# Batch 3's scaled memory sums transposed by the DMA crossbar from ScalarE's queue

## The chip, the cores and the metric

The kernel runs on one core of a Trainium2 chip. The core has four compute engines that matter here: TensorE (matmuls, with weight loads beside them), VectorE, ScalarE and GpSimd. Each works through its own queue of instructions in order. DMA transfers are issued by instructions too, from the queues of SyncE (SP), GpSimd and ScalarE. TensorE writes to PSUM, eight banks of it; VectorE and ScalarE read results from there.

The metric is the device time of one execution in microseconds, the median over several runs.

## The reference

Attention with learned memory slots, followed by a gated feed-forward block. Per batch (8) and head (8), with 576 positions, head size 64 and 32 memory slots:

```python
a = softmax(phi)                                  # over the 32 slots
k_m = np.einsum('bhsm,bhsd->bhmd', a, k)          # sums over the positions
v_m = np.einsum('bhsm,bhsd->bhmd', a, v)
attn = softmax(q @ k_m.T / sqrt(64))              # over the 32 slots
x = (attn @ v_m), heads side by side              # 4608 tokens x 512
out = (silu(x @ w_gate) * (x @ w_val)) @ w_out    # 512 -> 1536 -> 512
```

## The kernel before

The order of all instructions is written out by hand: an engine executes what the program emits for it, in the order of emission. Work goes batch by batch. The memory sums of batch b+1 are computed in the middle of the feed-forward work of batch b.

For one batch of the later six:

- **Sums and scaling.** `kv_sum` (L230) makes the sums k_m and v_m of all heads in two PSUM banks; `kv_norm` scales them on VectorE with the reciprocals of the softmax denominators (L266) into `t_bkv`, three blocks of 128x128 in bf16.
- **Transposition.** `kv_T` (L279 on) makes `t_kT`, the three blocks transposed. For batches 2 and 3 TensorE transposes them through the bank `p_T` (L288) and VectorE copies the bank out (L289). For batches 4 to 7 a DMA transposes them, issued from SP (L284).
- **The u round.** `u_round` (L472) multiplies v_m, from `t_kT`, with columns of the two weights w_gate and w_val. ScalarE (L492) and VectorE (L496) convert the result into `t_U`. The first u round of batch b+1 that reads the new `t_kT`, `u_three(b + 1)`, is emitted late in the stretch of batch b.
- **Scores.** `scores` (L396) multiplies k_m, also from `t_kT`, with q transposed (`t_qT`), at the start of the stretch of batch b+1. `t_qT` of batch 3 and later comes from another transposing DMA on SP (`load_qT`, L117).
- **Slots.** A stretch has 24 slots, one for each of 12 blocks of 128 hidden columns and each half of the positions. In slot s, `gv_gate` multiplies the gate (two matmuls, `p_g`, L515) and ScalarE applies silu (L532, `t_sg`), which frees the gate's bank. Then follow the two matmuls of the value of slot s-1 (`p_v`, L515) and its product with the silu on VectorE (L538, `t_h`), which frees the value's bank.
- **Banks.** `bank` takes the PSUM bank at the front of a list and `done` puts it at the end, both at the time of emission. What TensorE waits for, when it writes to a bank, is thus fixed by the order in the program.
- **Output products.** `products` (L723) multiply `t_h` and sums of it with w_out.

`spread` orders a stretch. Each stream of items gets a first and a last key, its items are put evenly between them, and all are emitted in the order of the keys. The 24 slots have the keys 0.5, 1.5, and so on. The two items of `kv_items(b + 1)`, the sums and then `kv_T`, run from `KV` = 6 to 10, so they have the keys 7 and 9; `u_three(b + 1)` has 19.5:

```python
            streams += [
                (kv_items(b + 1, lambda: (u_item(b, 2, "aava")(), run(take(2)))), KV, KV + 4),
                ([lambda: (u_three(b + 1), run(take(2)))], 19, 20),
            ]
        spread(*streams)
```

So `kv_T(3)` is emitted in the stretch of batch 2, after slot 8 and before slot 9. The sums' item ends with a u round of batch 2 (`u_item(b, 2, "aava")`: four banks, three converted on ScalarE and one on VectorE) ahead of slot 7.

Of the kernel before, what the change touches and what calls it, by code (L numbers as in the profile page):

```python
# [14 lines left out]
def kernel(  # L15
# [19 lines left out]
    nc = tc.nc  # L35
# [39 lines left out]
    def bank(shape, dtype, name):  # L75
        tag = free.pop(0)
        t = ps.tile(shape, dtype, tag=tag, name=name)
        held[id(t)] = tag, t
        return t

    def done(*tiles):

        for t in tiles:
            free.append(held.pop(id(t))[0])
# [83 lines left out]
    ephis, rSs, bkvs, kTs, es, atts = {}, {}, {}, {}, {}, {}  # L168
# [109 lines left out]
    def kv_T(b):  # L278


        kTs[b] = att.tile([128, 3, 128], BF16, tag="kT", name="t_kT")
        t = bkvs.pop(b)
        if b > 3:
            nc.sync.dma_start_transpose(out=kTs[b], in_=t.rearrange("p n x -> p (n x)"))  # L284
            return
        p = bank([128, 3, 128], BF16, "p_T")
        for n in (2, 0, 1):
            nc.tensor.transpose(p[:, n], t[:, n], ident)  # L288
        nc.vector.tensor_copy(out=kTs[b], in_=p)  # L289
        done(p)  # L290

    def kv_items(b, beside=None):


        def run_sums():
            o = 2 * D
            behind = b in esums and b != 3
            own = beside and not behind
            if own:
                d = bank([128, NG], FP32, "p_S")  # L300
                kv_denominators(b, d)
                kv_reciprocal(b, d)
                done(d)
            p = [bank([128, CH], FP32, f"p_kv{g}") for g in range(NG)]
            if not (own or behind):
                kv_denominators(b, p[0][:, o:o + NG])
            kv_sum(b, p, (0, 1))
            if behind:
                beside()
                kv_denominators(b, p[0][:, o:o + NG])  # L310
            if not own:
                kv_reciprocal(b, p[0][:, o:o + NG])
            kv_norm(b, p)
            if beside and not behind:
                beside()

        return [run_sums, lambda: kv_T(b)]
# [795 lines left out]
```

## Time and profile before

| | us |
|---|---|
| median of 3 runs (lowest, highest) | 232.76 (232.63, 233.4) |
| the profiled execution | 232.59 |
| its span, first to last instruction | 230.8 |
| TensorE busy | 222.3 (96%) |
| VectorE busy | 184.8 (80%) |
| ScalarE busy | 171.6 (74%) |
| GpSimd busy | 145.1 (63%) |

The granted TensorE clock is full in all forty slices of the page. The costliest groups are those of the slots: the matmuls of the gates and of the values (L515), 77.0 and 76.9 us, the products on VectorE (L538), 81.7 us in 192 instructions, and the silus on ScalarE (L532), 73.2 us in 192.

In the profile PE is TensorE's matmul row, PEld its weight loads, DVE is VectorE, ACT ScalarE, POOL GpSimd and SP SyncE; a `q` behind an engine (SPq, ACTq) marks what its queue issues, such as a DMA. Instructions in a row of the same kind are merged where they are shown in order of time, so a merged line's duration runs from the first start to the last end. Matmuls are pipelined: one that is listed with 0.29 us can be followed by the next after 0.12. What counts is the distance between starts.

### The profile page before, as it was taken

The page shows a single profiled execution, that of the slowest core. Times are in us where ns is not written, and L with a number is a line of the kernel's source. Part 1 is how long each engine was busy: PE and PEld are TensorE (multiplying, and loading weights), DVE is VectorE, ACT ScalarE, POOL GpSimd, SP SyncE. Part 2 cuts the span into 40 slices and gives each one's busy share as a digit, 9 for nine tenths or more (in the row PEclk, how much of TensorE's full clock was granted, in tenths as well). Part 3 has the DMA queues.
Part 4 walks back from the last instruction along what each step waited for, and adds up shares of the span by engine and source line. Part 5 has one row for each costly group of instructions (what it writes and reads, how often), then busy time and mean ns, then how long its engine had stood idle before and what let it go on. Part 6 is the DMA issues. An engine that isn't in the chain of part 4 may idle for free.

```text
span 230.8 us, 7191 instructions
## 1 busy us (share of the span) xinstructions
PE 222.3 (96%) x2818; PEld 169.7 (74%) x2818; DVE 184.8 (80%) x423; ACT 171.6 (74%) x365; POOL 145.1 (63%) x197
## 2 busy tenths in 40 slices
PE   6997799999999999999999999999999999999993
PEld 2554476778887777878788787887788778878882
DVE  4056789999976799989997668998999899977832
ACT  2858898988547989968896658978898789677310
POOL 8422427998099759765977689464845394029291
PEclk9999999999999999999999999999999999999999
DMA  6999999999996993999299964996022602202024
GB/s 213 209 211 206 199 207 207 216 250 266 207 210 176 258 257 69 224 204 177 78 214 195 230 137 110 253 231 101 18 76 102 116 0 95 87 7 91 23 93 162
DMA packets 36546, 36.84 MB, mean 160 GB/s; under 512 B 14496, under 2 KB 30880, under 8 KB 36512
## 3 DMA queue, kind: packets, MB, share of 16 engines
q0 software_dynamic: 16272, 22.42, 52.7%
q1 hardware_dynamic: 19712, 13.37, 22.8%
q10 hardware_dynamic: 528, 0.59, 0.8%
q8 instruction: 22, 0.36, 0.6%
q14 instruction: 12, 0.10, 0.1%
HBM read 42.47 MB, written 9.44 MB: 225 GB/s over the span
## 4 chain that ended last, share of the span: by engine, by line
PE 87%; DMA 9%; POOL 2%; issue 0%; DVE 0%; POOLq 0%
PE p_os L723 21%; PE p_g L515 21%; PE p_v L515 20%; PE p_oc L723 10%; DMA W<-in_moe_w_val_dram 9%; PE p_oa L723 5%; PE p_u L472 5%; PE p_kv L230 2%; PE p_g L396 1%; POOL t_kv L99 1%; POOL t_kv L103 1%; PE p_q L383 1%; POOL t_q L108 0%; POOL W L138 0%; DVE t_q L339 0%
## 5 line engine op out<-in xcount | busy, mean ns | idle before, releaser
L538 DVE TENSOR_TENSOR t_h<-t_sg,p_v 128x288 bf16<-128x288 bf16 x192 | 81.7, 451 | 14.3 <-PE p_v L515 7.3
L515 PEld LDWEIGHTS <-t_U 128*128 128x128 bf16 x768 | 73.9, 98 | 21.2 <-issue 3.5
L532 ACT ACTIVATE t_sg<-p_g 128x288 bf16<-128x288 f32 x192 | 73.2, 424 | 17.2 <-PE p_g L515 11.4
L515 PE MATMUL p_g<-t_A,t_U 128*128 128x288 bf16 x384 | 77.0, 286 | 0.0
L515 PE MATMUL p_v<-t_A,t_U 128*128 128x288 bf16 x384 | 76.9, 286 | 0.0
L723 PEld LDWEIGHTS <-t_S 128*128 128x128 bf16 x384 | 37.3, 98 | 4.5 <-issue 0.2
L603 POOL TENSOR_TENSOR t_S<-t_h 128x512 bf16<-128x512 bf16 x17 | 19.6, 1154 | 27.7 <-DVE t_h L538 26.4
L723 PEld LDWEIGHTS <-t_h 128*128 128x128 bf16 x288 | 27.1, 98 | 8.6 <-issue 5.0
L492 ACT CAST t_U<-p_u 128x512 bf16<-128x512 f32 x51 | 27.0, 606 | 6.4 <-PE p_u L472 6.4
L723 PE MATMUL p_os<-t_T,t_S 128*128 128x256 bf16 x192 | 23.7, 273 | 0.0
L560 POOL TENSOR_TENSOR t_S<-t_S,t_h 128x512 bf16<-128x512 bf16 x17 | 19.6, 1155 | 1.3
L560 POOL TENSOR_TENSOR t_S<-t_h 128x512 bf16<-128x512 bf16 x16 | 18.4, 1152 | 0.0
L560 POOL TENSOR_TENSOR t_S<-t_h,t_S 128x512 bf16<-128x512 bf16 x16 | 18.4, 1151 | 0.0
L472 PE MATMUL p_u<-W,t_kT 64*32 64x512 bf16 (+1 forms) x416 | 15.3, 363 | 1.2 <-DMA W<-in_moe_w_val_dram 0.6
L870 PE MATMUL p_warm<-bones 128*128 128x512 bf16 x44 | 13.6, 450 | 1.7 <-DVE bones L892 1.7
L496 DVE CAST t_U<-p_u 128x512 bf16<-128x512 f32 x21 | 13.6, 683 | 1.9 <-PE p_u L472 1.9
L723 PE MATMUL p_os<-t_T,t_h 128*128 128x256 bf16 x96 | 14.8, 273 | 0.0
L452 DVE TENSOR_TENSOR t_A<-t_E,t_lz 128x576 bf16<-128x576 bf16 x16 | 11.4, 739 | 0.7 <-ACT t_lz L428 0.7
L723 PE MATMUL p_oc<-t_T,t_S 128*128 128x256 bf16 x96 | 11.9, 273 | 0.0
L723 PE MATMUL p_oa<-WO,t_h 128*128 128x256 bf16 x96 | 11.8, 273 | 0.0
L723 PE MATMUL p_oc<-WO,t_S 128*128 128x256 bf16 x96 | 11.8, 273 | 0.0
L723 PE MATMUL p_os<-WO,t_h 128*128 128x256 bf16 x96 | 11.8, 273 | 0.0
(108 smaller groups left out, 312.5 us busy)
## 6 DMA issues: line engine op xcount, KB each, us to landing
out_dram<-t_o SPq DMA_DIRECT2D x11, 512.0 KB, 3.3
t_kv<-in_k_dram POOLq DMA_DIRECT2D x8, 576.0 KB, 10.7
t_q<-in_q_dram POOLq DMA_DIRECT2D x8, 576.0 KB, 8.7
t_kv<-in_v_dram POOLq DMA_DIRECT2D x8, 576.0 KB, 15.1
t_phi<-in_phi_dram POOLq DMA_DIRECT2D x6, 576.0 KB, 8.5
out_dram<-t_o SPq DMA_DIRECT2D x10, 256.0 KB, 3.8
WO<-in_moe_w_out_dram POOLq DMA_DIRECT2D x3, 512.0 KB, 19.4
W<-in_moe_w_gate_dram POOLq DMA_DIRECT2D x2, 512.0 KB, 16.5
```

Of the source, the lines that this page charges most:

```text
L230: nc.tensor.matmul(p[g][32 * i:32 * i + 32, 0:n], lhsT=phi_of(b, g, j, i), rhs=kvs[b][64 * g:64 * g + 64, w0:w1, i, j * D:(j + 1) * D], st ...
L452: nc.vector.tensor_tensor(out=a, in0=es.pop((b, g)), in1=lzs.pop((b, g)), op=ALU.mult)
L472: nc.tensor.matmul(p[g][32 * i:32 * i + 32, o:o + n], lhsT=kTs[b][64 * g:64 * g + 64, 2, 32 * i:32 * i + 32], rhs=w_part(w, c, i, g, halve ...
L492: nc.scalar.copy(out=t, in_=p)
L496: nc.vector.tensor_copy(out=t, in_=p)
L515: nc.tensor.matmul(p[:, 0:HALF], lhsT=Us[b, c, g][:, o // 2, which, 128 * (o % 2):128 * (o % 2 + 1)], rhs=atts[b, g][:, r], start=(g == 0) ...
L532: nc.scalar.activation(out=sg, in_=gate[:, 0:HALF], func=AF.Silu)
L538: nc.vector.tensor_tensor(out=dst, in0=sg, in1=val[:, 0:HALF], op=ALU.mult)
L560: eng.tensor_tensor(out=out, in0=x, in1=y, op=ALU.subtract)
L603: eng.tensor_tensor(out=t[:, 0], in0=A21, in1=A22, op=ALU.add)
L723: nc.tensor.matmul(mine[home][:, u], lhsT=lhs(c, m, u), rhs=rhs(c, m), start=fresh and u == 0, stop=(k == 5), skip_group_check=u == 1 or n ...
L870: nc.tensor.matmul(p[:, 0:128 * a], lhsT=bones, rhs=x.to_broadcast([128, a, 128]) if a > 1 else bones, start=True, stop=True,)
```

## The change

One condition and one choice of queue in `kv_T`:

```diff
         kTs[b] = att.tile([128, 3, 128], BF16, tag="kT", name="t_kT")
         t = bkvs.pop(b)
-        if b > 3:
-            nc.sync.dma_start_transpose(out=kTs[b], in_=t.rearrange("p n x -> p (n x)"))
+        if b > 2:
+            (nc.sync if b > 3 else nc.scalar).dma_start_transpose(out=kTs[b], in_=t.rearrange("p n x -> p (n x)"))
             return
         p = bank([128, 3, 128], BF16, "p_T")
```

For batch 3 the three TensorE transpositions, the bank `p_T` and VectorE's copy go away, and one transposing DMA of the whole `t_bkv` into `t_kT` is issued from ScalarE's queue, at the same place in the order of emission. Batches 2 and 4 to 7 stay as they are.

## The prediction

> **What bounds the kernel now.** I read first the page's strip of busy tenths and its chain of waits, then the view of one tile for the tiles of the edit, then the instructions in order of time from 79 to 91 us, where the step of batch 3 runs, and last SP's own instructions in order of time. The strip and the chain:
>
> ```profile
> PE   6997799999999999999999999999999999999993
> PE 87%; DMA 9%; POOL 2%; issue 0%; DVE 0%; POOLq 0%
> ```
>
> TensorE is full from the sixth slice on, and the list of waits on TensorE between 31 us and the end is empty. So TensorE has no slack that could swallow a delay: a microsecond in which it waits comes out at the end in full, and so does one that it saves. ScalarE (74%) and VectorE (80%) follow it and matter only where they hold a PSUM bank that TensorE wants.
>
> The tiles of the edit (least, median and greatest duration in ns, then first and last start in us):
>
> ```profile
> L288 PE MATMUL p_T<-ident,t_bkv x6: 219/219/219, 61.9 to 82.2; 128*128 128x128 bf16 x6
> L284 SPq DMA_TRANSPOSE t_kT<-t_bkv x4: 1179/1690/2255, 107.0 to 182.1; - x4
> L289 DVE COPY t_kT<-p_T x2: 350/354/357, 62.3 to 83.4; 128x384 bf16<-128x384 bf16 x2
> DMA to landing us min/median/max: 2.6/3.6/4.5
> ```
>
> Half of L288 and of L289 belong to batch 2 and stay. The four DMA rows are batches 4 to 7 on SP's queue: the same instruction that batch 3 now gets on ScalarE's.
>
> The place, in order of time (start, duration, engine and line; several instructions in a row are merged):
>
> ```profile
> 81.08 1.56 ACT L492 CAST t_U<-p_u 128x512 bf16<-128x512 f32 x3 [0.78 <-PE p_u L472]
> ...
> 81.64 0.41 PE L515 MATMUL p_g<-t_A,t_U 128*128 128x288 bf16 x2
> ...
> 82.13 0.33 PE L288 MATMUL p_T<-ident,t_bkv 128*128 128x128 bf16 x3
> ...
> 82.30 0.41 PE L515 MATMUL p_g<-t_A,t_U 128*128 128x288 bf16 x2
> ...
> 82.51 5.54 ACT L532 ACTIVATE t_sg<-p_g 128x288 bf16<-128x288 f32 x13
> ...
> 84.26 0.41 PE L515 MATMUL p_g<-t_A,t_U 128*128 128x288 bf16 x2
> ...
> 87.78 0.84 PE L472 MATMUL p_u<-W,t_kT 64*32 64x512 bf16 x24
> ...
> 89.69 1.35 ACT L532 ACTIVATE t_sg<-p_g 128x288 bf16<-128x288 f32 x4
> ```
>
> The gate at 81.64 is that of slot 8, the one at 82.30 of slot 9, and from there a slot takes 0.49 us, so that 84.26 is slot 13. ScalarE runs late here: its three casts end at 82.64, and the silu of slot 7, whose gate TensorE began at 81.14, starts at 82.51. Four silus back to back take 1.35 us and one takes 0.45, so their pitch is (1.35 - 0.45) / 3 = 0.30: slot 7 at 82.51, slot 8 at 82.81, slot 9 at 83.10 (narrower windows of the same view show these starts singly). The line at 87.78 is the first reader of the new t_kT.
>
> **What is removed.** TensorE: the three transpositions take the time from 82.13 to 82.30, so 0.17 us, on the path. VectorE: the copy, 0.35 us; VectorE isn't what TensorE waits for here, so I cost it at nothing. Its cover is TensorE's own pace; without it the copy would be worth up to 0.35. The PSUM bank p_T drops out of the rotation, which only moves who inherits which bank; that is followed below.
>
> **What is added, and where.** The items of one stretch are sorted by keys; the transposition has key 9, between slot 8 (8.5) and slot 9 (9.5). On ScalarE's queue it stands after the silu of slot 8 and ahead of the silu of slot 9. Its input t_bkv is complete at 81.80 (four scalings from 80.81 in 0.99 us on VectorE), so it finds its data ready and starts when ScalarE's queue reaches it: no sooner than about 82.85, just after the silu of slot 8 starts, and no later than about 83.3, when that one has ended. I take 83.1, where the next silu stood. That an issue holds what is behind it on ScalarE is seen at the start of the trace:
>
> ```profile
> 0.73 0.49 ACTq L94 DMA_DIRECT2D t_phi<-in_phi_dram  x1
> 1.26 1.28 ACT L857 ACT_TABLE_LOAD   x1 [1.26 <-PEq L1097]
> ```
>
> How long the issue takes on ScalarE (call it D) no row shows; the plain load there took 0.49 us against 0.45 on SP, so the engines are close to alike. From below D is 0.49, by that load. From above I use SP's four rows:
>
> ```profile
> 61.62 5.99 SPq L117 DMA_TRANSPOSE t_qT<-t_q  x1
> ...
> 106.98 2.25 SPq L284 DMA_TRANSPOSE t_kT<-t_bkv  x1
> ...
> 132.90 1.91 SPq L284 DMA_TRANSPOSE t_kT<-t_bkv  x1
> ...
> 158.28 1.47 SPq L284 DMA_TRANSPOSE t_kT<-t_bkv  x1
> ...
> 182.12 1.18 SPq L284 DMA_TRANSPOSE t_kT<-t_bkv  x1
> ```
>
> 1.18 belongs to a nearly idle DMA (share 0.11), 2.25 to one full of transfers. At 83 us the DMA share is above 1.1, loads and stores together. The eighteen-block transposition at 61.62, also beside loads, took 5.99 us against 4.03 in the idle DMA at 176.39, 1.49 times as much; 1.18 x 1.49 = 1.76. I take the median, 1.69, nearest to that, and keep 1.18 and 2.25 as ends.
>
> **What is queued behind it and who waits.** Behind the issue stand the silus of slots 9, 10 and on. Each frees a gate's bank for TensorE and feeds a product on VectorE. No output matmul (L723) runs from 76.2 to 90.7 us, so all eight banks rotate, and a slot takes two (gate, and the value of the slot before): a gate gets the bank of the gate four slots earlier. Without p_T, the eight banks from gate 9 to value 11 come from the four of the u round (last cast 82.64), gates 7 and 8 (silus ahead of the DMA) and values 6 and 7 (multiplied by 83.44). None of these is held up. Gate 13 is the first that needs a silu behind the DMA, that of slot 9.
> - Silu 9 starts at 83.1 + D + 0.04 (SP's next instruction starts 0.04 to 0.1 after such an issue) and lasts 0.45. A follower starts 0.04 after its end (the product of slot 7 at 82.99, its silu's end 82.95). Gate 13 can start at 83.63 + D.
> - Before it started at 84.26; without the transpositions TensorE is there at 84.09.
> - Net: D - 0.63, or -0.17 where D is under 0.46. With D = 1.69: **+1.06 us**. With 1.18: +0.55; with 2.25: +1.62. The start of the issue moves each by -0.25 to +0.2.
>
> After gate 13 nothing stops TensorE again: ScalarE catches up with 0.30 per silu against 0.49 per slot, and VectorE's products at 0.37 back to back (three from 79.42 in 1.18 us) too. The removed 0.17 is in this sum, since TensorE reaches the wait sooner and waits longer.
>
> **The landing.** t_kT must be there for the u round at 87.78, then at 88.84. From 83.1 with 2.6 to 4.5 us it lands at 85.7 to 87.6. Beside loads the large transpositions landed after 9.5 to 11.0 us and late in the kernel, without them, after 6.2: at most 1.77 times. On the 2.6 and 3.5 us of the late small ones (mean 3.05) that makes 5.4, and 88.5. Cost nothing; the cover is 0.3 to 3 us, and is gone only if the transfer takes over 5.7. The extra 0.1 MB delays loads that end near 88.3 and are first used by the sums at 102.67: nothing.
>
> **Rules.** The page "DMA: Bandwidth & Descriptors" of the Trainium skill, under "Issuing engines are not separate DMA queues", says that issuing from several engines saves only the sequencer's time, usually small beside the DMA. The rows differ: 1.69 of 3.6 us is 47%. Were the issue small, the sum would be -0.17; by the rows it is +1.06. The same page, under "Silent corruption: two transposing streams in flight at once", speaks against this change: transposes from ScalarE and from SP must wait for each other's completion. In this trace both such waits would be over before they begin (the last rival but one has the times), and the sum by the rule is the same +1.06.
>
> **The rivals.**
> - *Not slower: the issue is short and the banks hide it.* Where D is below 1.33, the four slots of bank lead eat the stop and the sum is under +0.7. At D = 0.49 it is -0.14, so 232.6; at 1.18 with an early start +0.3, 233.1. For it: the load issued in 0.49, the idle row, and ScalarE's ring being empty, where SP's had the long t_qT just ahead in all four rows. Against: the full DMA, and 5.99 against 4.03 on an SP that had issued nothing since 0.74.
> - *The landing decides.* If three queues share the engines (loads, stores until about 85, the transposition) and it takes over 5.7 us, the u round waits. At 6.5 us it lands at 89.6, 0.8 after the need: 1.06 + 0.8, so 234.6. Decides from 88.84. Against: the longest of its kind was 4.5.
> - *The issue waits for something in flight on SP's queue* (stores until about 85): ScalarE stands from 83.1 to 85.1, and the sum is +3.1, so 235.8. Nothing in the trace of before asks for such a wait: SP's last transposition ahead of it, issued at 61.62, landed 9.5 us later, at 71.1, and the next is issued at 100.22.
> - *The change moves nothing*, the issue overlapping silus: -0.17, 232.6.
>
> **The numbers.** The profiled execution took 232.59 us with a span of 230.8, near the median 232.76 of the runs; the sum puts the span at 231.9 and the median at 232.76 + 1.06 = 233.8. Chances: forecast 0.66 (its own range +0.3 to +1.8, of which 0.08 falls within 0.3%), short issue 0.18 (0.15 within, 0.03 at the edge of faster), late landing 0.10, wait on SP's transfers 0.04, nothing 0.02. What a measurement of this kernel tells from no change is about 0.3%, 0.7 us. So slower 0.58 + 0.10 + 0.04 = 0.72, same 0.08 + 0.15 + 0.02 = 0.25, faster 0.03: no part of the edit has 0.7 us to give on TensorE. The range runs from 232.8, inside the short issue, to 235.0, inside the late landing.
>
> **What would show it.** A ScalarE issue near 83 us of 1.2 to 2.3 us; the silu of slot 9 near 84.8; a TensorE wait for a silu of about one microsecond at the gate of slot 13, near 84.1; no wait at the u round; everything later shifted by the same amount to the end. I am wrong if ScalarE's silus run on through the issue, if the stop sits at the u round, or if the shift is given back later.

## The result and the profile after

The changed kernel takes 236.29 us (median of 6 runs, 235.73 to 237.45) against 232.79 us before: 3.5 us slower. The ratio of the runs is 1.0165, with a 95% interval of 1.0148 to 1.0182. The forecast was 233.8, the range ended at 235.0. The sign was right, but not for the reason given: the stop that was forecast did not come. The loss is over three times the size that was worked out, and it lies in other places.

The profiled execution took 236.49 us with a span of 234.7. Its strip and chain:

```profile
PE   7967899999999995999999999999999999999992
PE 83%; DMA 12%; POOL 2%; issue 0%; DVE 0%; POOLq 0%
```

TensorE has a hole in the slice at 88 to 94 us, and DMA's share of the chain grew from 9% to 12%. From 31 us on the list of TensorE's waits, which was empty before, has one line (total, times, longest), and the chain that ended last has a new piece in the same place (start, duration):

```profile
PE p_u L472 <- DMA t_kT<-t_bkv: 2.4, 1, 2.4
```

```profile
82.85 7.87 DMA t_kT<-t_bkv
```

The tile of the edit (least, median, greatest duration in ns, then starts; the landing is that of this one DMA):

```profile
L284 ACTq DMA_TRANSPOSE t_kT<-t_bkv x1: 1281/1281/1281, 82.9 to 82.9; - x1
...
DMA to landing us min/median/max: 7.9/7.9/7.9
```

The same stretch in order of time:

```profile
81.78 1.56 ACT L492 CAST t_U<-p_u 128x512 bf16<-128x512 f32 x3 [0.78 <-PE p_u L472]
...
82.84 0.41 PE L515 MATMUL p_g<-t_A,t_U 128*128 128x288 bf16 x2
82.85 1.28 ACTq L284 DMA_TRANSPOSE t_kT<-t_bkv  x1
...
83.22 0.74 ACT L532 ACTIVATE t_sg<-p_g 128x288 bf16<-128x288 f32 x2
...
84.24 4.36 ACT L532 ACTIVATE t_sg<-p_g 128x288 bf16<-128x288 f32 x11 [0.27 <-PE p_g L515]
...
84.80 0.41 PE L515 MATMUL p_g<-t_A,t_U 128*128 128x288 bf16 x2
...
87.98 0.41 PE L515 MATMUL p_v<-t_A,t_U 128*128 128x288 bf16 x2
...
90.77 0.84 PE L472 MATMUL p_u<-W,t_kT 64*32 64x512 bf16 x24 [2.37 <-DMA t_kT<-t_bkv]
```

Two things are to be seen. The issue (L284) begins at 82.85, while ScalarE's last cast still runs (to 83.34) and two silus ahead of it in the queue have not begun; they execute at 83.22 to 83.96, during the issue. And gates 9 to 13 go on in steps of 0.49 us (82.84 to 84.80): no stop at slot 13. The stop is at the u round, which waits from 88.40 to 90.77.

Matching TensorE's instructions of the two traces one by one gives the account of the profiled execution:

| stretch | later than before by, us | added there |
|---|---|---|
| start, up to 27 us (landings of the first loads) | 0.68 | 0.68 |
| from there to slot 8 | 0.71 | 0.03 |
| after the place of the three transpositions | 0.54 | -0.17 |
| after the u round's wait | 2.98 | 2.44 |
| last matmul | 2.99 | 0.01 |
| end of the span | 3.9 | 0.9 |

The 0.7 us at the start differ from run to run: in the profiles of the first three experiments below TensorE is 0.02, 0.23 and 0.05 us later at that point. The step of 2.44 and the 0.9 at the end are new with the change. The 0.9 us at the end shows in SP's waits, as a longer wait for the landing of the last store. Before:

```profile
SPq L1108 <- DMA out_dram<-t_q: 0.5, 1, 0.5
```

After:

```profile
SPq L1108 <- DMA out_dram<-t_q: 1.4, 1, 1.4
```

The store itself lands 2.1 us after its issue in both. What differs is its turn. In these traces the DMAs of SP and ScalarE use eight semaphores in rotation (a semaphore counts the landings), and at the end SP goes through all of them in a fixed order. Before, the last store had the last one, so the others were checked while it was under way. One DMA more puts it on the first, and the other checks and the close follow only after it: SP stands there until 232.87, and the span ends at 234.7, 1.8 us later, against 0.9 us from the landing (229.9) to the end before.

### The profile page after: what moved, and what is told of

Read it like the earlier page. It is cut to its first block, busy times and chain, and to the rows that moved or that the text cites. A ratio compares the mean times of both kernels' runs of the same rounds, so it can differ in the third digit from the quotient of the medians.

```text
span 234.7 us, 7186 instructions
## 1 busy us (share of the span) xinstructions
PE 221.3 (94%) x2815; PEld 169.3 (72%) x2815; DVE 185.0 (79%) x422; ACT 171.8 (73%) x365; POOL 145.3 (62%) x197
## 4 chain that ended last, share of the span: by engine, by line
PE 83%; DMA 12%; POOL 2%; issue 0%; DVE 0%; POOLq 0%
PE p_os L723 21%; PE p_g L515 19%; PE p_v L515 19%; PE p_oc L723 10%; DMA W<-in_moe_w_val_dram 9%; PE p_oa L723 5%; PE p_u L472 5%; DMA t_kT<-t_bkv 3%; PE p_kv L230 2%; PE p_g L396 1%; POOL t_kv L99 1%; POOL t_kv L103 1%; PE p_q L383 1%; POOL t_q L108 0%; POOL W L138 0%
## 5 line engine op out<-in xcount | busy, mean ns | idle before, releaser
L870 PE MATMUL p_warm<-bones 128*128 128x512 bf16 x44 | 12.4, 418 | 1.7 <-DVE bones L892 1.7
```

The source lines that it names most:

```text
L870: nc.tensor.matmul(p[:, 0:128 * a], lhsT=bones, rhs=x.to_broadcast([128, a, 128]) if a > 1 else bones, start=True, stop=True,)
```

## The experiments

Two theories of the wait: the transposition's packets meet the loads and stores in flight (traffic), or ScalarE's queue serves such a DMA worse than SP's (queue). A third is about the end (tail).

**1. From SP's queue.**

```diff
-            (nc.sync if b > 3 else nc.scalar).dma_start_transpose(out=kTs[b], ...)
+            nc.sync.dma_start_transpose(out=kTs[b], ...)
```

> Theory A (traffic): in the changed kernel the transposition landed 7.9 us after its issue because its 416 small packets take turns with the loads and stores in flight; the issuing queue does not matter. Then from SP's queue it lands 6.5 to 8 us after its issue too, TensorE waits 2 to 3 us at the u round that reads t_kT, and the time stays near 236 us. Theory B (queue): ScalarE's queue serves such a DMA later than SP's. Then from SP it lands after 2.6 to 4.5 us, as batches 4 to 7 do, TensorE does not wait, and the time is near 233.5 us.

235.81 us (235.41 to 237.79), ratio 1.0155 (1.0126 to 1.0184). The tile:

```profile
L284 SPq DMA_TRANSPOSE t_kT<-t_bkv x1: 1193/1193/1193, 82.0 to 82.0; - x1
...
DMA to landing us min/median/max: 7.7/7.7/7.7
```

```profile
PE p_u L472 <- DMA t_kT<-t_bkv: 2.0, 1, 2.0
```

From SP it lands as late, and TensorE waits 2.0 us. It isn't the queue. ScalarE, with nothing to issue, loses nothing here, and yet the time is that of the changed kernel within its spread. By this trace the choice of ScalarE costs at most the 0.4 us by which the wait is shorter here.

**2. The reader later.** The u round of batch 3 moves from slot 19 to behind the next six output units.

```diff
         else:
             run(take(6))
+            if b == 3:
+                u_three(3)
...
-                ([lambda: (u_three(b + 1), run(take(2)))], 19, 20),
+                ([lambda: (b > 2 and u_three(b + 1), run(take(2)))], 19, 20),
```

> The transposition as in the changed kernel, but the first reader of t_kT (the u round of batch 3) stands after the slots and the next six output units, some 3 us later in TensorE's work. If the wait for the landing (2.4 us) is the main loss, it shrinks to under 0.5 us, and some 2 to 2.4 us come back: about 234 us. If the loss comes from ScalarE being held by the issue, moving the reader gives nothing back: about 236 us.

235.21 us (235.04 to 235.37), ratio 1.0104 (1.0091 to 1.0117). The DMA lands 8.0 us after its issue, and nothing waits for it any more; but the reader's place costs in its turn. Scores and conversions now crowd each other, and TensorE has four new waits from 92 us on:

```profile
PE p_g L396 <- DVE t_U L496: 0.5, 1, 0.5
PE p_u L472 <- DVE t_U L496: 0.3, 1, 0.3
PE p_oa L723 <- DVE t_U L496: 0.2, 1, 0.2
PE p_v L396 <- ACT t_U L492: 0.2, 1, 0.2
```

So only about 1 us came back where 2 were expected. That the wait for the landing went is clear; as a repair it is half a miss.

**3. The tail alone.** The kernel before, with one small load that nobody reads.

```diff
     load_phi(1, nc.scalar)
+    tiny = consts.tile([1, 64], FP32, tag="tiny", name="tiny")
+    nc.sync.dma_start(out=tiny, in_=moe_w_out[0:1, 0:64])
```

> The kernel before with one more DMA of 256 bytes on SP at the very start, whose data nobody reads. Theory C (tail): one more DMA on SP's and ScalarE's queues moves the last store to the first of the eight DMA semaphores, whose wait comes first among the waits at the end, so that all the others are gone through after it: the span between the last store's issue and the end grows by 0.9 us and the time is 233.6 to 233.8 us. Rival: the longer tail of the changed kernel was chance, and the time stays at 232.8 us.

233.63 us (233.54 to 234.1), ratio 1.0040 (1.0028 to 1.0052): 0.88 us more, from a DMA of 256 bytes two hundred microseconds earlier. TensorE's last matmul is where it was, and SP's wait at the end is that of the changed kernel:

```profile
SPq L1110 <- DMA out_dram<-t_q: 1.4, 1, 1.4
```

The tail is shown. It is the place of the last store's semaphore that counts, not the number of DMAs: in the traces of experiment 5 below one DMA more on these queues moves the last store from the seventh place to the eighth, and from its landing to the end it takes 0.92 us instead of 0.98; without the stores of batch 1 it holds the fourth, and that takes 1.16. On the first place it takes 1.8 to 1.9. No run takes one store away from the changed kernel.

**4. The loads later.** GpSimd issues batch 4's loads only once `t_kT` is there.

```diff
                     sums[1, c](part)
-            loads(4)
...
+        if b == 2:
+            streams += [([lambda: (wait_for(kTs[3][0:1, 0, 0:1]), loads(4))], 9, 10.2)]
```

> The changed kernel, but the loads of batch 4 are issued by GpSimd only once t_kT has landed, so that the transposition meets stores alone. Theory A: it lands within 3 to 5 us of its issue, TensorE does not wait at the u round, and the time falls by 2 us or more to about 234 us, if the later loads cost nothing themselves. Theory B: it lands after 7 us or more all the same.

242.55 us (242.04 to 243.49), ratio 1.0424 (1.0406 to 1.0442): slower still, but the transposition itself does what the traffic theory says. Its landing, and the packets in flight on all queues between 83 and 85 us (packets, MB, share of 16 engines):

```profile
DMA to landing us min/median/max: 2.4/2.4/2.4
```

```profile
q10 hardware_dynamic: 416, 0.10, 24.1%
```

With the queues otherwise empty the first packet starts 1.3 us after the issue and the last packet of data 0.6 us after that. TensorE doesn't wait at the u round of batch 3. The condition in the expectation, that the later loads cost nothing, failed. GpSimd issues them from 88.8 instead of 72.7 us on, and now batch 4's transposition, on SP, lands 5.6 us after its issue. TensorE waits 5.4 us there, and the granted clock (the third figure from the end of a line) is halved for 3.4 us after it. With a wait of 1.4 us for GpSimd, the 1.7 us that the half clock costs and the 0.9 of the tail that makes 9.4 of the 9.8 us by which the span is longer:

```profile
PE p_u L472 <- DMA t_kT<-t_bkv: 5.4, 1, 5.4
```

```profile
112.50:113.00 0.50, 0.50 (x7) 0.35 (x4) 0.47 (x2) 0.21 (x1) 0.50 (x2) 1.00 1.17 191
118.60:120.00 1.40, 1.38 (x24) 0.32 (x24) 0.65 (x1) 0.69 (x2) 1.38 (x2) 0.50 0.44 53
...
122.00:124.00 2.00, 2.00 (x19) 1.64 (x17) 1.85 (x5) 1.61 (x5) 0.00 (x0) 1.00 1.01 320
```

**5. A probe in place of the transposition.** What makes 7.9 us out of 2.4 was taken apart with a plain DMA that nobody waits for, issued from ScalarE at the same place, in a base where every transposition is TensorE's. The base replaces `load_qT` and the DMA of `kv_T` by `q_T` (as a stream of its own) and the lines L286 to L290 of the kernel before; the probe:

```diff
+        if b == 3:
+            x = consts.tile([128, 3, 256], BF16, tag="probe", name="t_probe")
+            nc.scalar.dma_start(out=x[:, :, 0:128], in_=t)     # 384 pieces of 256 bytes
```

The others copy one block (`x[:, 2, 0:128]` from `t[:, 2]`, 128 pieces of 256 bytes) or into a dense tile (128 pieces of 768 bytes), leave out the stores of batch 1's output, or have `b == 7`.

The base:

> A base for the next three: the kernel before with every transposition, those of q and of the memory sums, on TensorE, so that no transposing DMA is left. TensorE has some 90 more transpositions of 128x128 (18 for each of five batches, at 0.05 to 0.06 us each) and 12 more for the sums: some 6 us, 238 to 240 us. The loads of batch 4 run from 73 to 88 us as in the kernel before.

384 pieces:

> The base with a plain DMA that nobody waits for, issued from ScalarE's queue where the transposition of batch 3 stood: t_bkv copied within SBUF in 384 pieces of 256 bytes. Theory A (a first packet some 4 us after the issue beside loads, then one packet in turn with each load packet, 135 a microsecond): it lands 6 to 7.5 us after its issue. Rival (the delay belongs to the transposing kind of DMA): it lands within 3 us. In both the time is that of the base within 0.3 us, if ScalarE's issue is covered by work queued ahead of it, apart from up to 0.9 us at the end by where the last store's semaphore stands.

128 pieces:

> As the last, with one block of the three: 128 pieces of 256 bytes. Theory A: two thirds of the turns are saved, so it lands 1.5 to 2 us sooner than the 384 pieces, 4.5 to 5.5 us after its issue. Rival (a fixed delay): the same landing as with 384 pieces.

768 bytes each:

> The bytes of the 384 pieces in 128 pieces of 768 bytes. If turns are taken by the packet, it lands like the 128 small pieces, 4.5 to 5.5 us after its issue; if the engines share by bytes, like the 384 pieces, 6 to 7.5 us.

Without the stores:

> The probe of 384 pieces, with the stores of batch 1's output left out (those that SP issues from 73 to 78 us and that are written until about 85.5 us). If the first packet is late because of the stores, it comes 1 to 2 us after the issue and the landing is at 5 to 6 us; if the loads alone delay it, the first packet still comes 3.4 to 4 us after the issue, as that of the large transposition at 61.6 us did beside loads alone, and the landing stays at 7 to 8 us.

At batch 7:

> The probe of 384 pieces at the same place of the stretch before batch 7, where no loads are in flight. Theory A: the first packet comes about 1.1 us after the issue, the 384 packets take under 1 us, and it lands 2 to 3 us after its issue. Rival: a DMA of this shape takes 7 to 8 us whatever runs beside it.

The base takes 239.53 us (ratio 1.0292, 1.0261 to 1.0323), as worked out. The probes of batch 3 (239.18, 239.69, 239.61 and, without the stores, 239.57 us, one run each) and that of batch 7 (239.85) are within 0.4 us of it: ScalarE's issue costs nothing that shows. Four of the landings as the view of the tile has them, first the 384 pieces, then those at batch 7, then 128 pieces of 256 bytes and 128 of 768:

```profile
L279 ACTq DMA_DIRECT2D t_probe<-t_bkv x1: 693/693/693, 82.2 to 82.2; - x1
...
DMA to landing us min/median/max: 7.9/7.9/7.9
```

```profile
L279 ACTq DMA_DIRECT2D t_probe<-t_bkv x1: 692/692/692, 187.9 to 187.9; - x1
...
DMA to landing us min/median/max: 2.2/2.2/2.2
```

```profile
L279 ACTq DMA_DIRECT2D t_probe<-t_bkv x1: 525/525/525, 82.6 to 82.6; - x1
...
DMA to landing us min/median/max: 5.8/5.8/5.8
```

```profile
L279 ACTq DMA_DIRECT2D t_probe<-t_bkv x1: 525/525/525, 82.6 to 82.6; - x1
...
DMA to landing us min/median/max: 5.9/5.9/5.9
```

All of them, with the DMA packets of the traces sorted by queue (packets of data only; each DMA adds 16 or 32 of 4 bytes):

| DMA | beside it | first packet after, us | from first to last packet, us | landed after, us |
|---|---|---|---|---|
| transposition, changed kernel | loads and stores | 4.0 | 3.4 | 7.9 |
| transposition from SP (1) | loads and stores | 3.9 | 3.2 | 7.7 |
| 384 pieces | loads and stores | 4.1 | 3.3 | 7.9 |
| 128 pieces | loads and stores | 3.9 | 1.4 | 5.8 |
| 128 pieces of 768 bytes | loads and stores | 3.9 | 1.5 | 5.9 |
| 384 pieces, no stores | loads, most of them until 85 us | 2.4 | 1.5 | 4.4 |
| 384 pieces, batch 7 | nothing | 1.3 | 0.5 | 2.2 |
| transposition, loads later (4) | nothing | 1.3 | 0.6 | 2.4 |

The first three probes land 0.3 to 0.4 us later than the expected spans end; the one without stores, at 4.4 us, lands sooner than either reading of it had. The table settles three points. The delay is not of the transposing kind: a plain copy in as many pieces lands just as late. It has two parts: some 4 us before the first packet, for 128 pieces as for 384, where idle queues need 1.3, and then a turn for every packet, whatever its bytes. And both parts come from what else is in flight. What the 4 us are made of stays open: in all six traces beside loads and stores the first packet starts within 0.4 us of the stores' last one, which may be chance. Without the stores it starts after 2.4 us; but there most of the loads are through 3.5 us sooner than in the base, so that row does not tell loads from stores. A mean packet of the loads takes 0.1 us on its engine. In the changed kernel from 82.8 to 86.8 us no packet of queue 10, ScalarE's, is there:

```profile
q0 software_dynamic: 492, 0.55, 80.0%
q1 hardware_dynamic: 253, 0.45, 34.7%
```

and from 86.8 to 90.2 us:

```profile
q0 software_dynamic: 396, 0.44, 74.7%
q10 hardware_dynamic: 413, 0.10, 22.4%
```

413 packets (383 of them of 256 bytes, the others of 4) against 396 of the loads: about one each in turn. The 384 packets of data in 3.4 us are 113 per microsecond, against 384 in 0.6 us with idle queues. One each is not a rule for every DMA: in the kernel before, from 65.17 to 67.00 us, the packets of the large transposition (q1) go beside loads (q0) nearly five to one, and why is not shown.

```profile
q1 hardware_dynamic: 563, 0.14, 88.9%
q0 software_dynamic: 120, 0.12, 39.7%
```

The Trainium skill, page "DMA: Bandwidth & Descriptors", section "Queues, rings and completion order", says that each engine goes round the queues that have work and takes a whole packet, typically of some 9 to 17 descriptors, from one before it turns to the next. The 413 against 396 agree with turns; whether a packet of this trace is a packet or a descriptor in the page's sense, no run shows.

## Why the prediction was wrong

**The bound and the removed work: right.** TensorE takes any wait over in full: the 2.44 us at 90 us are still there at the last matmul. The three transpositions were worth 0.17 us, as worked out.

**The issue on ScalarE: a term of +1.06 us that is not there.** D was taken as 1.69 and is 1.28, inside its ends. The larger error is the start. The step put it between 82.85 and 83.3 "when ScalarE's queue reaches it". In the changed kernel it begins at 82.85, but TensorE is 0.71 us later there, so in the time of the kernel before that is 82.14, a microsecond sooner than the 83.1 taken. The issue did not wait for the work ahead of it to be done. It begins 0.10 us after the gate of slot 8 ends (82.76), for which the silu ahead of it waits; in all seven traces with an issue from ScalarE at this place it is 0.04 to 0.10 us. At batch 7 it begins 0.03 us after its data are there. So it ran beside 1.1 us of casts and silus. What is behind it does wait: silu 9 started at 84.24, 0.1 us after the issue's end. (The line shown for this in the prediction names another releaser, PEq L1097.) It ended at 84.65, and gate 13 stood at 84.80: the four slots of bank lead were just enough. The rival of the short issue had the bank lead right, with 0.18, and the last rival the overlap with the silus, with 0.02.

**The landing: the step that failed.** "On the 2.6 and 3.5 us of the late small ones (mean 3.05) that makes 5.4, and 88.5. Cost nothing." It was 7.9. Stretching a total by the ratio of two other totals treats the delay as one factor. It is a first packet late by some 3 us, which a small DMA pays as fully as a large one, plus a turn per packet. The first part could have been read in the trace of before: the large transposition issued at 61.62 us beside loads has its first packet 3.55 us later. The second could not. At the pace of that transposition beside loads (225 to 407 packets per microsecond in 65.17 to 67.00 us) 384 packets take 0.9 to 1.7 us, and from the last packet of the late small ones to their landing it is 0.7 to 0.8; the sum is 5.2 to 6.1, on both sides of the 5.7 from which the wait was said to begin. With the 3.4 us that turns of one for one take, as the changed kernel and the probes show, it is 7.7. So the rival of the late landing deserved far more than 0.10; it had the mechanism and the place, and priced the landing at 6.5 us. That its 5.7 us nearly holds is luck. TensorE would have been at the u round at 88.32, 5.5 us after the issue began: the need came 1.2 us sooner than taken, without the stop at gate 13, and the issue 1.0 us sooner.

**The tail: missing altogether.** The text followed TensorE up to the last matmul and not beyond. One DMA more among those that share eight semaphores put the last store on the first of them, and cost 0.9 us at the end, a quarter of the loss.

**The sum.** -0.17 for TensorE's transpositions, +2.44 for the landing, +0.9 for the tail: +3.2, or 236.0. Measured are 236.29, and 235.73 to 236.49 in four of six runs. The other two, 237.41 and 237.45, show a mean granted clock of 0.989 and 0.990 against 0.995 to 0.997. A spell of 3.4 us at half clock, as in experiment 4 after a wait of 5.4 us, would take 0.5 x 3.4 / 236 = 0.7% off the mean and cost 1.7 us, which fits both. Two of the six runs of experiment 1 have such a clock too (237.04 and 237.79 us, 0.991), and no listed run of the kernel before or of experiments 2 and 3 has one under 0.995. But no trace of these runs exists, so this stays argued. The Trainium skill, page "TensorE: Matmul & The Clock Gate", section "Part 1: The HAM clock gate", says that a window of some 3.4 us with TensorE idle halves the clock and that the windows run freely. Experiment 4 shows such a spell (0.50 after a wait of 5.4 us). A wait of 2.4 us is shorter than such a window, and in the changed kernel's profile it did not bring one; so the page's rule speaks rather against this reading.

**What is not shown.** No run splits the transposition so that the block that the u round reads goes first; the probe of 128 pieces landed 2.1 us sooner than that of 384, which is less than the wait of 2.44. No version faster than the kernel before was found, and on TensorE there was only 0.17 us to win.

## What to carry to other kernels

Price a small DMA by the traffic at its moment: the delay of a first packet, read from another DMA issued into such traffic, plus its packets at the pace of one turn each with the packets beside them (113 per microsecond here), and compare that with the time its first reader comes. A TensorE transposition that costs 0.06 us, off the DMA queues, is hard to beat while loads run. When the number of DMAs changes, look at the end of the program too: which semaphore the last store holds, and what is checked after it.

## What was not expected of the hardware

- A DMA issue on ScalarE starts and runs while earlier instructions of ScalarE are still executing: 1.28 us of issue beside 1.1 us of casts and silus. Only what is behind it waits.
- Beside loads and stores the first packet starts about 4 us after the issue, for 128 pieces as for 384, from ScalarE as from SP; into idle queues after 1.3 us.
- 128 pieces of 768 bytes land like 128 of 256 bytes (5.9 and 5.8 us), and 384 of 256 bytes after 7.9: beside these loads the number of packets counts, not the bytes.
- A DMA of 256 bytes at the start lengthens the kernel by 0.88 us at the end, through the place of the last store's semaphore in the order of the last waits.
